# Rectifying the experts' first layer through a 32-bit buffer in SBUF, and scaling a routing table on another engine

## The chip, the cores and the metric

The kernel runs on one core of one Trainium2 chip. The metric is the device time of one execution in microseconds (us). Before the change it is 1554.09 us, the median of 3 runs (1553.83 to 1555.44). A core has a matrix engine (TensorE, shown as PE, its weight loads as PEld), a vector engine (VectorE, DVE), an engine for functions (ScalarE, ACT), a general one (GpSimd, POOL) and one that issues transfers (SyncE, SP). Each takes its own instructions strictly in order and waits for others by semaphores. SBUF is the working memory. TensorE writes its results to PSUM.

## What is computed

Attention with decay, then a dense layer pair, then a mixture of experts. Only the last matters here:

```python
logits = x @ w_gate                      # 4608 tokens, 8 experts
order = np.argsort(-logits.flatten())    # each token goes to the best expert that is not full (576 places)
for e in range(8):
    mask = assigned == e
    h = np.maximum(x[mask] @ w1[e], 0.0) # 576 x 1024
    out[mask] = h @ w2[e]                # 576 x 512
```

## The kernel before

The first two thirds of the time, to about 1016 us of the trace, are attention and the dense layers. The experts follow in `phase_c`. Matrix products are in 32 bits of which TensorE takes a shorter form (`fp32r`), so every factor is split into a high part (a copy into `fp32r`) and a low part (the value less its high part). A product is then three: high by high, low by high, high by low.

`experts(r)` (before: lines 1137 to 1200) does one expert, and is called for r from 0 to 7. Its first layer has eight steps f, one for 128 of the 1024 hidden columns. A step has 24 matmuls (L1158) into two PSUM buffers of 288 tokens each, `ps[0]` and `ps[1]`. These come from the pool `psF` with four buffers, so that step f+2 writes the buffers of step f. After its matmuls a step issues: two ACT instructions that rectify each half of PSUM straight into the high part `hh` (L1167); then `split_w(r, 2, f)`, which splits one block of the second layer's weights, the high part `w2h` by ACT (L1074) and the low part `w2l` by POOL (L1075). The low part of the rectified step is a function `low`, kept in the list `late`. It is called in the next step after the sixth matmul (j == 5), or after the eighth step. It issues three DVE instructions of 288, 224 and 64 columns (L1171), each of which reads PSUM again, rectifies, and subtracts `hh`. The second layer (L1189) uses `hh`, `hl`, `w2h` and `w2l` of f = 0 to 7 for each of five blocks of tokens; its results go to SBUF by ACT (L1194, L1196) and out by an indirect transfer on POOL.

While one expert is computed, the routing finds the tokens of a later one. `route(r)` is a generator whose pieces are issued between the matmuls of the experts: after each matmul pair a clock in the program is advanced by a constant (`TK1`, `TK2`), and a piece is issued when the clock has passed a time set by constants (`Y_...`). So the order on every engine is fixed when the program is built. A round of routing finds a threshold in six steps. A step compares on DVE (`cmp`, L839, L908 or L925), counts on PE (L930 or L934), goes on on DVE (`ca`, L938), on PE (L949, L950), and again on DVE (`d`, `dm`, `tr`, L957 to L960, whose result `pi` sets the next threshold). Then comes the choice of an expert (`GG`, L969; PE L973, L975; `nn`, `mx`, `X`, L979 to L988; PE L995) and the list of its tokens: a table `b1` (0 or 1, 128x720, bf16) by DVE (L1018), its product with a constant per partition, into one half of `R`, by ACT (L1019), a table `A` by DVE (L1021), the other half of `R` by DVE (L1023), and their products on PE (L1027). Routing 0 comes before the first expert; routings 1 to 7 lie beside experts 0 to 6.

`SB` holds small tables of the routing in one PSUM bank (its tile is named `st` in the trace), and `F` constants in SBUF (`tf`).

Of the kernel before, what the change touches and what calls it, by code (L numbers as in the profile page):

```python
# [9 lines left out]
F32 = mybir.dt.float32  # L10
# [8 lines left out]
AF = mybir.ActivationFunctionType  # L19
OP = mybir.AluOpType  # L20
# [6 lines left out]
E, FE, CAP = 8, 1024, 576  # L27
# [721 lines left out]
def phase_c(tc, ctx, w1, w2, rtf, rti, rth, rtb, x2d, L, out):  # L749
    nc = tc.nc  # L750
# [3 lines left out]
    fp = ctx.enter_context(tc.tile_pool(name="fp", bufs=1))  # L754
# [4 lines left out]
    V = nc.vector  # L759
# [7 lines left out]
    F = {k: tf[:, a:b] for k, (a, b) in RF.items()}  # L767
# [4 lines left out]
    def bc(ap, axis, n):  # L772
        shape = list(ap.shape)
        shape.insert(axis, n)
        return ap.unsqueeze(axis).to_broadcast(shape)

    def rt(shape, dt, name, bufs=1):
        return rp.tile(shape, dt, tag=name, name=name, bufs=bufs)
# [62 lines left out]
    def route(r):  # L841
# [29 lines left out]
        if r < E - 1:  # L871
# [6 lines left out]
            for half in range(2):  # L878
# [7 lines left out]
                for s, (shift, J) in enumerate(STEPS):  # L886
# [58 lines left out]
                    for i in range(nj):  # L945
                        o = pd[:, 8 * nc_ * i:8 * nc_ * i + 8 * nc_]
# [8 lines left out]
                    if not fast:  # L955
# [5 lines left out]
                                           op0=OP.is_ge, op1=OP.mult, accum_out=pi)  # L961
# [54 lines left out]
        b1 = rt([128, NCOL, 20], BF16, "b1")  # L1016
        R = rt([128, NCOL, 2, 20], BF16, "R")
        V.tensor_tensor(b1, bc(zh, 2, 20), bc(F["i20"], 1, NCOL), op=OP.is_equal)  # L1018
        nc.scalar.activation(R[:, :, 1, :], b1, AF.Copy, scale=F["p"])  # L1019
        yield Y_Z  # L1020
        V.tensor_tensor(A, bc(zl, 2, 32), bc(F["i32"], 1, NCOL), op=OP.is_equal)  # L1021
        yield 1.4
# [42 lines left out]
    def load_w2(r, f):  # L1065
        if f < 8:
            WS[r, 2, f] = wp.tile([128, KC, 128], F32, tag="ws2", name="ws2", bufs=3)
            nc.sync.dma_start(out=WS[r, 2, f], in_=w2[bass.ds(EV[r], 1), f].rearrange("e p k m -> (e p) k m"))

    def split_w(r, i, f):  # L1070
        s = WS.pop((r, i, f))
        h = wp.tile([128, KC, 128], F32R, tag=f"w{i}h{f}", name=f"w{i}h{f}")
        l = wp.tile([128, KC, 128], F32R, tag=f"w{i}l{f}", name=f"w{i}l{f}")
        nc.scalar.activation(h, s, AF.Copy)  # L1074
        nc.gpsimd.tensor_tensor(l, s, h.bitcast(F32), op=OP.subtract)  # L1075
        (W1 if i == 1 else W2)[f] = h, l
# [42 lines left out]
    def each(f):  # L1119
        for r in range(E):  # L1120
            for d in f(r):
                yield d

    threads = [[0.0, each(f)] for f in (route, weights, tokens)]
    clock = [0.0]

    def tick(dt):
        clock[0] += dt
        for th_ in threads:
            while th_[1] is not None and th_[0] <= clock[0]:  # L1130
                d = next(th_[1], None)
                if d is None:
                    th_[1] = None
                else:
                    th_[0] = clock[0] + d * (YS[len(IDX) > 1] if th_ is threads[0] else YS[0])

    def experts(r):
        while r not in XT:
            tick(0.2)
        xh, xl = XT.pop(r)  # L1140
        idx = IDX[r]
        H, late = [], []
        load_w2(r, 0)
        load_w2(r, 1)
        for f in range(8):
            load_w2(r, f + 2)
            ps = [psF.tile([128, 512], F32, tag="ff", name="ff")[:, :288] for _ in range(2)]
            while f not in W1:
                tick(0.2)
            w1h, w1l = W1.pop(f)  # L1150
            prods = [(w, xh, k) for k in range(KC) for w in (w1h, w1l)] + [(w1h, xl, k) for k in range(KC)]
            seq = [(i, u) for i in range(12) for u in range(2)]
            if r == 0 and f == 0:

                seq = [(i, u) for a, b in ((0, 8), (8, 12)) for u in range(2) for i in range(a, b)]
            for j, (i, u) in enumerate(seq):
                w, x, k = prods[i]
                nc.tensor.matmul(ps[u], w[:, k, :], x[:, k, 288 * u:288 * u + 288], start=i == 0, stop=i == 11)  # L1158
                if j % 2:
                    tick(TK1)  # L1160
                if late and j == 5:
                    late.pop()()

            hh = fp.tile([128, CAP + 64], F32R, tag=f"hh{f}", name="hh")
            hl = fp.tile([128, CAP - 64], F32R, tag=f"hl{f}", name="hl")
            for u in range(2):
                nc.scalar.activation(hh[:, 288 * u:288 * u + 288], ps[u], AF.Relu)  # L1167

            def low(ps=ps, hh=hh, hl=hl):
                for a, b, o in ((0, 288, hl[:, :288]), (288, 512, hl[:, 288:]), (512, 576, hh[:, 576:])):  # L1170
                    V.scalar_tensor_tensor(o, ps[a // 288][:, a % 288:a % 288 + b - a], 0.0, hh[:, a:b].bitcast(F32),  # L1171
                                           op0=OP.max, op1=OP.subtract)
            late.append(low)
            H.append((hh, hl))
            split_w(r, 2, f)
            first_done[r] = f == 7
        late.pop()()
        for t in (0, 4, 1, 2, 3):
            n = min(128, CAP - 128 * t)
            ps = psF.tile([128, 512], F32, tag="ff", name="ff")  # L1180
            for f in range(8):
                w2h, w2l = (w.rearrange("p k m -> p (k m)") for w in W2[f])
                hh = H[f][0][:, 128 * t:128 * t + 128]
                if t < 4:
                    prods = (ps, hh, w2h), (ps, H[f][1][:, 128 * t:128 * t + 128], w2h), (ps, hh, w2l)
                else:
                    prods = (ps, hh, w2h), (ps[:n], hh[:, :n], w2l)
                for i, (o, h, w) in enumerate(prods):
                    nc.tensor.matmul(o, h, w, start=f == 0 and i == 0, stop=f == 7 and i == len(prods) - 1,  # L1189
                                     skip_group_check=t == 4)  # L1190
                    tick(TK2)
            o = fp.tile([128, DM], F32, tag="o", name="o", bufs=3)
            if t < 4:
                nc.scalar.activation(o, ps, AF.Copy)  # L1194
            else:
                nc.scalar.activation(o[:n], ps[n:], AF.Copy)  # L1196
                V.tensor_tensor(o[:n], ps[:n], o[:n], op=OP.add)
            nc.gpsimd.indirect_dma_start(out=out, out_offset=bass.IndirectOffsetOnAxis(ap=idx[:n, t:t + 1], axis=0),
                                         in_=o[:n], in_offset=None)
# [20 lines left out]
    for r in range(E):  # L1220
        experts(r)
# [82 lines left out]
```

## Time and profile before

| what | value |
|---|---|
| median of 3 runs | 1554.09 us (1553.83 to 1555.44) |
| the profiled execution | 1556.99 us, its span 1555.1 us, so 1.9 us around it |
| PE, share of the span | 94%, 1456.5 us |
| DVE | 73%, 1132.7 us |
| ACT | 49%, 761.5 us |
| POOL | 36%, 558.3 us |
| chain that ended last: PE, DVE, issue, ACT, POOL | 73%, 14%, 4%, 3%, 2% |
| mean granted TensorE clock | 0.973 of full speed |

The profile shows one execution. Busy time is the time in which an engine had an instruction under way; the chain that ended last is followed back from the last instruction to whatever released each one. In the views below a row names the line, the engine, the operation, what it writes and reads (`hl<-ff,hh`), partitions by elements and types, and how many there were.

### The profile page before, as it was taken

Reading aid. Unit: us, or ns where it says so; the run is one execution under the profiler, and the core shown is the slowest. Engines: PE = TensorE matmul, PEld = TensorE weight load, DVE = VectorE, ACT = ScalarE, POOL = GpSimd, SP = SyncE. Lnnn points to the kernel's source line nnn. Section 1 sums busy time; section 2 is a strip of 40 time slices with the busy share of each in tenths; the row PEclk is TensorE's granted clock in tenths of the full one; section 3 lists DMA queues with packets and bytes.
Section 4 is the critical chain, followed back from the end, with each engine's and each line's share of the span. In section 5 each row is a group of like instructions: output and inputs, shape, how many; then the busy total and the mean of one; then the engine's idle time right before and its main releaser. Section 6 shows DMA issues by size and latency. Waiting matters only on the chain.

```text
span 1555.1 us, 26174 instructions
## 1 busy us (share of the span) xinstructions
PE 1456.5 (94%) x9500; PEld 1276.3 (82%) x9500; DVE 1132.7 (73%) x2740; ACT 761.5 (49%) x1585; POOL 558.3 (36%) x492
## 2 busy tenths in 40 slices
PE   5989899899999999999999999937999999999997
PEld 4777788789898989898989898825788887887996
DVE  7999965878787878777878787867776766765210
ACT  4767775455656565656564646503333323323421
POOL 4546541212222221212121223224535535446541
PEclk7999999999999999999999999967999999999999
DMA  7522222111111111111111100013423423426210
GB/s 258 197 72 82 82 104 74 43 62 42 62 41 62 42 62 42 62 41 62 42 54 50 43 22 21 1 37 129 125 85 124 129 85 120 130 84 193 91 65 31
DMA packets 48610, 122.43 MB, mean 79 GB/s; under 512 B 6624, under 2 KB 13408, under 8 KB 48224
## 3 DMA queue, kind: packets, MB, share of 16 engines
q1 hardware_dynamic: 41184, 99.80, 19.2%
q0 software_dynamic: 6144, 19.93, 4.0%
q8 instruction: 75, 1.23, 0.3%
q10 hardware_dynamic: 1152, 1.02, 0.2%
q14 instruction: 55, 0.45, 0.1%
HBM read 101.85 MB, written 18.87 MB: 78 GB/s over the span
## 4 chain that ended last, share of the span: by engine, by line
PE 73%; DVE 14%; issue 4%; ACT 3%; POOL 2%; DMA 1%; SPq 0%; POOLq 0%; DVEq 0%; ACTq 0%
PE h L426 22%; PE x L489 21%; PE ff L1189 11%; PE ff L1158 10%; PE pb L290 2%; PE pb L357 2%; PE pb L369 1%; DVE work L208 1%; DVE t L456 1%; DVE t L450 1%; DVE junk L530 1%; DVE t L452 1%; PE tp L1112 1%; PE pb L305 1%; DVE h L454 1%
## 5 line engine op out<-in xcount | busy, mean ns | idle before, releaser
L470 POOL TENSOR_TENSOR gl<-t,gh 128x384 fp32r<-128x384 f32 x192 | 200.2, 1043 | 652.6 <-ACT gh L467 565.8
L426 PE MATMUL h<-xh,w0h 128*128 128x384 f32 x704 | 240.4, 341 | 11.8 <-DVE t L456 11.6
L426 PE MATMUL h<-xh,w0l 128*128 128x384 f32 x704 | 238.3, 338 | 0.0
L436 ACT ACTIVATE S<-h 128x384 f32<-128x384 f32 x192 | 93.7, 488 | 286.7 <-PE h L426 286.5
L489 PE MATMUL x<-w1h,gh 128*128 128x512 f32 x576 | 231.2, 401 | 0.5 <-ACT gh L467 0.5
L489 PE MATMUL x<-w1l,gh 128*128 128x512 f32 x576 | 226.9, 394 | 0.0
L489 PE MATMUL x<-w1h,gl 128*128 128x512 f32 x576 | 217.0, 395 | 1.3 <-POOL gl L470 1.0
L450 DVE SCALAR_TENSOR_TENSOR t<-t,S 128x384 f32<-128x384 f32 x192 | 114.1, 594 | 128.7 <-ACT t L439 128.1
L530 DVE SCALAR_TENSOR_TENSOR junk<-x2r,wg 128x512 f32<-128x512 f32 x240 | 168.7, 703 | 5.2
L426 PE MATMUL h<-xl,w0h 128*128 128x384 f32 x704 | 152.6, 338 | 0.0
L426 PEld LDWEIGHTS h<-xh,w0h 128*128 128x128 f32 x704 | 132.7, 188 | 23.4 <-DVE t L456 12.3
L1075 POOL TENSOR_TENSOR w2l<-ws,w2h 128x512 fp32r<-128x512 f32 x64 | 82.6, 1293 | 161.4 <-ACT w2h L1074 161.4
L426 PEld LDWEIGHTS h<-xh,w0l 128*128 128x128 f32 x704 | 133.1, 189 | 6.7
L489 PEld LDWEIGHTS x<-w1h,gl 128*128 128x128 f32 x576 | 108.1, 188 | 29.7 <-POOL gl L470 5.7
L1189 PE MATMUL ff<-w2h,hh 128*128 128x512 f32 x320 | 127.5, 399 | 3.1 <-DVE hl L1171 2.0
L456 DVE COPY_PREDICATED t<-m,h 128x384 f32<-128x384 uint16 x192 | 114.4, 596 | 20.9 <-ACT m L445 1.7
L1189 PE MATMUL ff<-w2l,hh 128*128 128x512 f32 (+1 forms) x320 | 127.4, 398 | 0.6 <-POOL w2l L1075 0.6
L489 PEld LDWEIGHTS x<-w1h,gh 128*128 128x128 f32 x576 | 108.6, 188 | 22.9 <-ACT gh L467 1.3
L426 PEld LDWEIGHTS h<-xl,w0h 128*128 128x128 f32 x704 | 126.7, 189 | 0.3 <-DVE xl L413 0.2
L439 ACT ACTIVATE t<-S,bias 128x384 f32<-128x384 f32 x192 | 118.3, 616 | 17.4 <-POOL gl L470 0.9
L489 PEld LDWEIGHTS x<-w1l,gh 128*128 128x128 f32 x576 | 108.6, 189 | 17.1
L1158 PE MATMUL ff<-xh,w1h 128*128 128x288 f32 x512 | 115.0, 302 | 6.3 <-DVE hl L1171 5.5
(212 smaller groups left out, 2989.6 us busy)
## 6 DMA issues: line engine op xcount, KB each, us to landing
ws<-in_w SPq DMA_DIRECT2D x128, 256.0 KB, 2.8
ain<-in_qkv SPq DMA_DIRECT2D x36, 768.0 KB, 4.2
wst<-in_wio SPq DMA_DIRECT2D x32, 512.0 KB, 3.5
x2d<-x2r SPq DMA_DIRECT2D x33, 256.0 KB, 2.0
w1h<-in_qkv SPq DMA_DIRECT2D x12, 192.0 KB, 4.6
w1l<-in_qkv SPq DMA_DIRECT2D x12, 192.0 KB, 3.5
w0h<-in_qkv SPq DMA_DIRECT2D x12, 192.0 KB, 4.0
w0l<-in_qkv SPq DMA_DIRECT2D x12, 192.0 KB, 4.1
```

The lines of the kernel that those rows point to most:

```text
L290: nc.tensor.matmul(PSA[k][a][:, chunk(c)], kt[r, chunk(c)], q[r, chunk(c)], start=True, stop=True)
L426: nc.tensor.matmul(h[:, :TB], w[0][f][:, hp, :], x, start=i == 0, stop=i == 11)
L436: nc.scalar.activation(S, h, AF.Square, scale=KSC)
L439: nc.scalar.activation(AT[s][2], AT[s][1], AF.Square, bias=bias[:, 0:1])
L450: nc.vector.scalar_tensor_tensor(t, t, PA - PB * PB / 4, S, op0=OP.add, op1=OP.mult)
L456: nc.vector.copy_predicated(t, m.bitcast(U16), h)
L470: nc.gpsimd.tensor_tensor(G[s][1], TT.pop(s), G[s][0].bitcast(F32), op=OP.subtract)
L489: nc.tensor.matmul(X2[n][i], g[:, i * 128:i * 128 + 128], w, start=(f == 0 and g is gh and w is wh), stop=(f == NF - 1 and g is gl))
L530: nc.vector.scalar_tensor_tensor(j, r, 1.0, wg[e // 4][:, e % 4, :], op0=OP.mult, op1=OP.mult, accum_out=L[:, c, e:e + 1])
L1075: nc.gpsimd.tensor_tensor(l, s, h.bitcast(F32), op=OP.subtract)
L1158: nc.tensor.matmul(ps[u], w[:, k, :], x[:, k, 288 * u:288 * u + 288], start=i == 0, stop=i == 11)
L1189: nc.tensor.matmul(o, h, w, start=f == 0 and i == 0, stop=f == 7 and i == len(prods) - 1, skip_group_check=t == 4)
```

## The change

In the first layer the two ACT instructions write 32-bit values to a new SBUF tile `raw` (two buffers). A third ACT instruction copies all 576 columns of it to the high part. `low` then is two DVE instructions, of 512 and 64 columns, which subtract `hh` from `raw`; they no longer read PSUM. In the routing, for every round but the first, the product of `b1` with a constant per partition goes from ACT to DVE.

```diff
@@ route
         V.tensor_tensor(b1, bc(zh, 2, 20), bc(F["i20"], 1, NCOL), op=OP.is_equal)
-        nc.scalar.activation(R[:, :, 1, :], b1, AF.Copy, scale=F["p"])
+        if r:
+            V.tensor_scalar(R[:, :, 1, :], b1, F["p"], None, op0=OP.mult)
+        else:
+            nc.scalar.activation(R[:, :, 1, :], b1, AF.Copy, scale=F["p"])
@@ experts
             hl = fp.tile([128, CAP - 64], F32R, tag=f"hl{f}", name="hl")
+            raw = fp.tile([128, CAP], F32, tag="raw", name="raw", bufs=2)
             for u in range(2):
-                nc.scalar.activation(hh[:, 288 * u:288 * u + 288], ps[u], AF.Relu)
-
-            def low(ps=ps, hh=hh, hl=hl):
-                for a, b, o in ((0, 288, hl[:, :288]), (288, 512, hl[:, 288:]), (512, 576, hh[:, 576:])):
-                    V.scalar_tensor_tensor(o, ps[a // 288][:, a % 288:a % 288 + b - a], 0.0, hh[:, a:b].bitcast(F32),
-                                           op0=OP.max, op1=OP.subtract)
+                nc.scalar.activation(raw[:, 288 * u:288 * u + 288], ps[u], AF.Relu)
+            nc.scalar.activation(hh[:, :CAP], raw, AF.Copy)
+
+            def low(raw=raw, hh=hh, hl=hl):
+                for a, b, o in ((0, 512, hl), (512, 576, hh[:, 576:])):
+                    V.tensor_tensor(o, raw[:, a:b], hh[:, a:b].bitcast(F32), op=OP.subtract)
             late.append(low)
```

The order of PE, POOL and SP is the same as before. ACT has 57 instructions more (64 copies, less 7 products of the routing). DVE has 57 fewer (64 less, 7 more).

DVE in expert 1, the low part of step f = 4 between two pieces of the routing (`ca` and `d`). Before:

```order
L938 TENSOR_TENSOR ca<-rt,tf 128x32
L1171 SCALAR_TENSOR_TENSOR hl<-ff,hh 128x288
L1171 SCALAR_TENSOR_TENSOR hl<-ff,hh 128x224
L1171 SCALAR_TENSOR_TENSOR hh<-ff,hh 128x64
L957 TENSOR_REDUCE d_12053<-rt 128x16
```

And with the change:

```order
L938 TENSOR_TENSOR ca<-rt,tf 128x32
L1176 TENSOR_TENSOR hl<-raw,hh 128x512
L1176 TENSOR_TENSOR hh<-raw,hh 128x64
L957 TENSOR_REDUCE d_12066<-rt 128x16
```

The place in the queue is the same; two instructions stand for three, and both operands are now in SBUF.

ACT at the end of expert 1's first layer (steps f = 6 and 7). Before:

```order
L1167 ACTIVATE hh<-ff 128x288 x2
L1074 ACTIVATE w2h_12158<-ws_11966 128x512
L1019 ACTIVATE R<-b_12189,tf 128x36x20
L1167 ACTIVATE hh<-ff 128x288 x2
L1074 ACTIVATE w2h_12218<-ws_12026 128x512
```

And with the change:

```order
L1171 ACTIVATE raw<-ff 128x288 x2
L1172 ACTIVATE hh<-raw 128x576
L1077 ACTIVATE w2h_12174<-ws_11979 128x512
L1171 ACTIVATE raw<-ff 128x288 x2
L1172 ACTIVATE hh<-raw 128x576
L1077 ACTIVATE w2h_12235<-ws_12040 128x512
```

The routing's product is gone from ACT's queue, where it stood ahead of step 7's rectifying; a copy stands between rectifying and the weights' split.

DVE at the same place, around the tables of the routing. Before:

```order
L1018 TENSOR_TENSOR b_12189<-st,tf 128x720
L1171 SCALAR_TENSOR_TENSOR hl<-ff,hh 128x288
L1171 SCALAR_TENSOR_TENSOR hl<-ff,hh 128x224
L1171 SCALAR_TENSOR_TENSOR hh<-ff,hh 128x64
L1171 SCALAR_TENSOR_TENSOR hl<-ff,hh 128x288
L1171 SCALAR_TENSOR_TENSOR hl<-ff,hh 128x224
L1171 SCALAR_TENSOR_TENSOR hh<-ff,hh 128x64
L1021 TENSOR_TENSOR A<-st,tf 128x1152
L1023 TENSOR_TENSOR R<-b_12189,st 128x36x20
```

And with the change:

```order
L1018 TENSOR_TENSOR b_12205<-st,tf 128x720
L1020 TENSOR_SCALAR R<-b_12205,tf 128x36x20
L1176 TENSOR_TENSOR hl<-raw,hh 128x512
L1176 TENSOR_TENSOR hh<-raw,hh 128x64
L1176 TENSOR_TENSOR hl<-raw,hh 128x512
L1176 TENSOR_TENSOR hh<-raw,hh 128x64
L1024 TENSOR_TENSOR A<-st,tf 128x1152
L1026 TENSOR_TENSOR R<-b_12205,st 128x36x20
```

The product now stands right behind the table that it reads, ahead of the low parts of steps 6 and 7.

## Rows read from the trace of the kernel before

**Rows 1.** Busy time by stage: engine busy us (instructions), granted clock, DMA share, GB/s

```profile
1120.00:1160.00 40.00, 38.64 (x311) 33.91 (x310) 26.77 (x81) 11.25 (x25) 16.33 (x15) 1.00 0.29 89
```

**Rows 2.** Waits of PE from 1075 us: us in total, times, longest

```profile
PE ff L1158 <- DVE hl L1171: 5.5, 6, 2.0
PE ff L1189 <- DVE hl L1171: 2.0, 2, 1.1
PE tp L1112 <- DVE xl L1115: 1.4, 1, 1.4
PE ff L1189 <- ACT w2h L1074: 1.1, 1, 1.1
```

**Rows 3.** Waits of ACT from 1075 us: us in total, times, longest

```profile
ACT hh L1167 <- PE ff L1158: 122.2, 53, 3.9
...
ACT R L1019 <- DVE b L1018: 33.0, 7, 6.8
```

**Rows 4.** Groups by shape from 1060 us: count | busy us, mean ns | idle before

```profile
L1167 ACT ACTIVATE hh<-ff 128x288 fp32r<-128x288 f32 x128 | 45.6, 408 | 125.6 <-PE ff L1158 125.5
L1074 ACT ACTIVATE w2h<-ws 128x512 fp32r<-128x512 f32 x64 | 40.6, 634 | 0.0
...
L1171 DVE SCALAR_TENSOR_TENSOR hl<-ff,hh 128x288 fp32r<-128x288 f32 x64 | 29.0, 453 | 58.9 <-ACT hh L1167 58.9
...
L1115 DVE TENSOR_TENSOR xl<-tp,xh 128x512 fp32r<-128x512 f32 x32 | 21.6, 687 | 26.9 <-ACT xh L1114 22.2 <-issue 3.1 <-ACT R L1019 1.5
```

**Rows 5.** Single lines over the span: count: ns min/median/max, first and last start

```profile
L450 DVE SCALAR_TENSOR_TENSOR t<-t,S x192: 537/555/1674, 48.0 to 1009.2; 128x384 f32<-128x384 f32 x192
...
L470 POOL TENSOR_TENSOR gl<-t,gh x192: 1000/1018/1524, 53.2 to 1012.4; 128x384 fp32r<-128x384 f32 x192
...
L1075 POOL TENSOR_TENSOR w2l<-ws,w2h x64: 1278/1293/1323, 1077.5 to 1521.6; 128x512 fp32r<-128x512 f32 x64
```

**Rows 6.** DVE and POOL in order of time, near 126 us: start and length, us

```profile
125.73 0.68 DVE L226 SCALAR_TENSOR_TENSOR work<-wst,work 128x512 f32<-128x512 f32 x1
126.13 1.17 POOL L470 TENSOR_TENSOR gl<-t,gh 128x384 fp32r<-128x384 f32 x1 [2.93 <-ACT gh L467]
126.34 1.51 DVE L237 TENSOR_TENSOR w1l<-work,w1h 128x512 fp32r<-128x512 f32 x1
```

**Rows 7.** The same view near 121 us and near 208 us

```profile
120.60 1.02 POOL L470 TENSOR_TENSOR gl<-t,gh 128x384 fp32r<-128x384 f32 x1
120.62 1.41 DVE L450 SCALAR_TENSOR_TENSOR t<-t,S 128x384 f32<-128x384 f32 x1 [1.74 <-ACT t L439]
...
208.34 0.68 DVE L226 SCALAR_TENSOR_TENSOR work<-wst,work 128x512 f32<-128x512 f32 x1
208.38 1.52 POOL L470 TENSOR_TENSOR gl<-t,gh 128x384 fp32r<-128x384 f32 x1 [1.42 <-issue]
```

**Rows 8.** In order of time, expert 1, step f = 4 of the first layer

```profile
1154.16 0.71 ACT L1167 ACTIVATE hh<-ff 128x288 fp32r<-128x288 f32 x2 [2.52 <-PE ff L1158]
1154.61 0.76 DVE L1171 SCALAR_TENSOR_TENSOR hl<-ff,hh 128x288 fp32r<-128x288 f32 x2 [0.49 <-ACT hh L1167]
...
1155.48 1.28 POOL L1075 TENSOR_TENSOR w2l<-ws,w2h 128x512 fp32r<-128x512 f32 x1 [2.46 <-ACT w2h L1074]
...
1155.98 0.23 DVE L957 TENSOR_REDUCE d<-rt 128x16 f32<-128x64 f32 x1 [0.48 <-PE rt L950]
...
1157.70 0.75 DVE L969 TENSOR_TENSOR GG<-P,st 128x576 bf16<-128x576 bf16 x1
...
1158.81 0.42 PE L973 MATMUL rt<-GG,tb 128*128 128x192 bf16 x3
```

**Rows 9.** In order of time, the end of expert 1's first layer

```profile
1165.24 0.90 ACT L1019 ACTIVATE R<-b,tf 128x720 bf16<-128x720 bf16 x1 [2.91 <-DVE b L1018]
...
1168.53 0.89 DVE L1023 TENSOR_TENSOR R<-b,st 128x720 bf16<-128x720 bf16 x1
...
1170.56 0.66 PE L1027 MATMUL rt<-R,A 128*128 128x160 bf16 x7
```

## The prediction

> **What bounds the kernel now.** I read the stages first. In the stretch of the experts, PE is busy 38.6 of 40 us, DVE 26.8, ACT 11.3 and POOL 16.3, with the clock granted in full [rows 1]. So PE sets the time there, and a change on the other engines counts only through PE's waits. I read these next. From 1075 us on PE waits 5.5 + 2.0 us for `hl`, the low part whose reading of PSUM sets a buffer free, 1.4 us for `xl`, and 1.1 us for `w2h` [rows 2]: 10.0 us, nearly all that the change could remove. Behind most of it stands one thing: ACT waits 33.0 us, in seven places, with the routing's product at the head of its queue until DVE has made the table `b1` [rows 3], and the rectifying of the next step waits behind it. The reader is to see that the change aims at these waits. What it can cost has to come from the routing: its pieces on DVE and PE are interleaved in a fixed order with the experts, so a DVE that runs late stops PE at the next routing matmul.
>
> **What the change does, part by part.**
>
> *ACT.* 64 copies of 576 columns are added. A copy of 512 takes 634 ns [rows 4], so I take 0.7 us each, some 45 us in all (0.63 to 0.75 us each is the bound). They are hidden in throughput: ACT waits 122.2 us for the first layer's matmuls before it rectifies, in 53 places [rows 3]. They are not hidden in delay: `hh`, and so the low part, is ready 0.8 us later (0.7 and a wait of about 0.1 us of ACT for its own result). Where that cover is gone, which is where the routing's product now stands, the product leaves too. `w2h` and with it POOL's `w2l` also come 0.8 us later. PE waited for `w2h` once, 1.1 us [rows 2], where ACT was held by the routing's product; else the 21 matmuls of steps 0 to 6 of the second layer stand ahead of step 7's weights. I cost the delay at nothing; without that cover it would be 0.8 us in each of 8 experts, 6.4 us.
>
> *PSUM.* A buffer is free when ACT has rectified it, no longer when DVE has subtracted. The 7.5 us of waits for `hl` lose their reason. ACT now waits for DVE if `raw`'s two buffers are full, one whole step later than PE did. What is late next is DVE.
>
> *DVE's low part.* Three instructions become two. The old ones cost 453 ns for 288 columns, and by 687 ns for 512 [rows 4] a column is about 1.04 ns. A subtraction of 512 columns that has both operands in SBUF takes 0.68 us undisturbed [rows 6], 64 columns more by that slope 0.2. So the work is about the same. The Trainium skill ("VectorE: DVE Perf Modes", The TRN2 errata) prices a result from SBUF at 58 cycles and its columns, from PSUM at 120; by that the large part would take an estimated 0.59 us and run 0.06 us shorter than from PSUM, where the rows show 0.68 against 0.69. The rows decide; by the page the 64-column part would start before POOL's `w2l`, and the sum would be that of the second rival below.
>
> *The port.* This is the point on which the forecast rests. A DVE instruction that reads two operands from SBUF is stopped by a POOL instruction that does so, and stops it. L450 takes 555 ns at the median and up to 1674, POOL's L470 1018 and up to 1524; `w2l`, in the experts, where the low parts read PSUM, never leaves 1278 to 1323 [rows 5]. The order decides: DVE that starts 20 ns after POOL takes 1.41 us, DVE that starts 40 ns before it makes POOL take 1.52 [rows 7]. Between two DVE instructions that follow each other POOL gets in: one began at 125.73, POOL at 126.13 took 0.15 us more than its 1.02 (so the first held it for 0.55 us), and the second, 0.61 us after the first, ended 0.55 us after POOL [rows 6]. The Trainium skill says this too ("SBUF — State Buffer", Who interferes with whom): the shared port goes to whichever instruction starts first, for its whole length; it speaks against this change, and the trace agrees.
>
> *One step worked out.* Expert 1, step 4 [rows 8]: the two rectifyings end at 1154.87. The copy ends at C = 1155.65. The 512-column part starts 0.04 us later (the first rectifying, 408 ns [rows 4], ends at 1154.57, and DVE started at 1154.61), so at 1155.69; the 64-column part 0.61 us behind it at C + 0.65. `w2l` came 0.61 us after the rectifyings and now comes at C + 0.61, 0.04 us before the 64 columns. By [rows 7] POOL wins, and DVE stands until 1155.65 + 0.61 + 1.29 + 0.1 = 1157.65. Behind it stands `d`, before at 1155.98: 1.67 us late. From `d` to the end of `GG` is 2.47 us, so `GG` ends at 1160.1; PE came for it at 1158.81. PE stops for 1.3 us.
>
> *The sum of the stops.* I went through the 48 low parts of experts 0 to 5 in this way, each from where DVE stood behind the rectifying. 33 cost nothing: DVE's next instruction waited for PE anyway, or PE came over 1 us later. The others, in us: expert 0: 1.3, 1.7, 2.1; expert 1: 0.3, 1.3, 1.0; expert 2: 1.1, 0.8, 0.4; expert 4: 0.9, 1.3, 1.0; expert 5: 0.7, 0.4, 0.3. Together 14.6 us. Experts 6 and 7 have no routing in their first layers, and DVE idles there: nothing.
>
> *The routing's product.* DVE has no such row; its cheapest neighbour would be some 0.3 us, its dearest is the other half of `R` at 0.89 [rows 9]. I take 0.6, as it has one operand in SBUF and no second. It frees ACT's queue, and PE would reach the end of a first layer earlier. But there the routing's own matmul L1027 comes, and DVE must have `A` and `R` ready. In expert 1 `R` ends at 1169.42 and PE takes it at 1170.56 [rows 9]: 1.1 us to spare. With the change the product and the two low parts, with step 7's `w2l` between the two halves, move `A` and `R` by 1.2 us, so nothing of PE's 1.6 us there is kept. By the same working the places at L1027 give, in us: expert 0 -0.9, 1 +0.1, 2 +0.6, 3 -1.6, 4 -0.2, 5 +0.3, and the wait for `xl` in expert 6 -1.0. Together -2.7.
>
> *Sum.* 14.6 - 2.7 = 11.9 us more. On the profiled execution of 1556.99 us that is 1568.9; it lies 2.9 us above the median of the three runs, so I forecast **1566 us**. The stops are uncertain by about half a microsecond each in common, and the product by 0.3 us in six places, so this case spans 1558 to 1574.
>
> **The rivals.**
>
> *The 64 columns slip in first.* The margin is 0.04 us, and DVE 40 ns ahead wins [rows 7]. Then the common case costs only the copy's delay, most of which PE's lateness covers. There remain 3.8 us of stops, where the low part starts late and falls into `w2l`, against about 3.7 us gained: 1554 us, 1551 to 1558. For it: the margin is no larger than what I can read. Against it: two instructions that follow each other let POOL in [rows 6].
>
> *No stop at the port worth speaking of, and the waits go.* If POOL's start misses the low part (because ACT splits the weights later than I think, or DVE gets the 64 columns through as part of the first) and the routing has more slack than I read, the 10.0 us of [rows 2] go, less 1.5 us for the copy's delay and about 2.5 us which the routing's own matmuls take back: 6 us less, 1548, 1544 to 1551. It decides from the point where the low part ends no later than about 1 us after it does now. For it: PE's waits are real, and PSUM is freed without DVE. Against it: [rows 5], where the same two engines stop each other by up to a whole instruction.
>
> **How the numbers follow.** A measurement of this kernel can tell about 0.2% from no change, 3.1 us. The forecast has 0.60, all of it slower by more than that. The first rival has 0.20: 0.14 within, 0.04 slower, 0.02 faster. The second has 0.20: 0.19 faster, 0.01 within. So faster 0.21, same 0.15, slower 0.64. The range of 1548 to 1573 leaves out about half of the second rival and a little of the forecast's upper end.
>
> **What would show it.** Right: `w2l` still near 1.29 us, but the 64-column subtraction with a median far over 0.2 us, near 1.3 where DVE was free; waits of PE for `GG`, `cmp` and `X` of the routing in place of those for `hl`; ACT's 33.0 us wait gone; L1027 waiting for `R`. Wrong: subtractions of 0.68 and 0.2 us throughout; waits of PE for the routing no longer than now; or `w2l` stretched to 1.9 us, which would mean that DVE goes first. The forecast falls if the 64 columns are not held in most steps.

## The result, and the profile after

The changed kernel takes 1568.86 us (median of 5 runs, 1567.58 to 1570.11), the kernel before on the same chip 1554.77 (1553.83 to 1555.82): 1.0088 times as long, 95% interval 1.0075 to 1.0102. It is slower by 14.1 us.

The part that the change touches runs from the first to the last matmul `ff`. It took 475.4 us before (1070.4 to 1545.8 us) and takes 490.7 us now (1066.9 to 1557.6), 15.3 us more; the part ahead of it, which the change leaves as it is, was 3.5 us shorter in this execution (over the twelve traces of this case the first `ff` starts at 1064.8 to 1070.4 us). One stretch of it by stages, which answers to [rows 1] and has its columns:

```profile
1120.00:1160.00 40.00, 38.05 (x317) 33.86 (x316) 29.94 (x75) 15.99 (x32) 15.61 (x15) 1.00 0.27 86
```

DVE does fewer instructions than before (75 for 81) and is busy for 29.94 us, where it was 26.77. So its instructions have become longer. Which ones, the view of single lines says (as [rows 5]; L1176 is the low part, L1020 the product, L1172 the copy, L1078 the weights' low part):

```profile
L1176 DVE TENSOR_TENSOR hl<-raw,hh x64: 679/692/1794, 1074.3 to 1533.4; 128x512 fp32r<-128x512 f32 x64
L1176 DVE TENSOR_TENSOR hh<-raw,hh x64: 210/1311/1339, 1074.9 to 1534.1; 128x64 fp32r<-128x64 f32 x64
L1020 DVE TENSOR_SCALAR R<-b,tf x7: 407/407/421, 1106.9 to 1435.8; 128x720 bf16<-128x720 bf16 x7
L1172 ACT ACTIVATE hh<-raw x64: 682/686/688, 1073.6 to 1532.7; 128x576 fp32r<-128x576 f32 x64
L1078 POOL TENSOR_TENSOR w2l<-ws,w2h x64: 1265/1287/1813, 1074.9 to 1534.0; 128x512 fp32r<-128x512 f32 x64
```

64 columns take 210 ns undisturbed and 1311 at the median, more than the 512 columns ahead of them and as long as one `w2l` of POOL, whose own median has not moved. The place worked out ahead, expert 1's step f = 4, shows why; in order of time, as [rows 8]:

```profile
1153.61 0.71 ACT L1171 ACTIVATE raw<-ff 128x288 f32<-128x288 f32 x2 [2.61 <-PE ff L1161]
...
1154.36 0.69 ACT L1172 ACTIVATE hh<-raw 128x576 fp32r<-128x576 f32 x1
...
1155.08 0.69 DVE L1176 TENSOR_TENSOR hl<-raw,hh 128x512 fp32r<-128x512 f32 x1 [1.51 <-ACT hh L1172]
...
1155.64 1.29 POOL L1078 TENSOR_TENSOR w2l<-ws,w2h 128x512 fp32r<-128x512 f32 x1 [3.28 <-ACT w2h L1077]
1155.68 1.33 DVE L1176 TENSOR_TENSOR hh<-raw,hh 128x64 fp32r<-128x64 f32 x1
...
1156.93 0.21 DVE L957 TENSOR_REDUCE d<-rt 128x16 f32<-128x64 f32 x1
```

POOL starts 0.04 us ahead of the 64 columns and ends at 1156.93; these end 0.08 us behind it, at 1157.01. Behind them stand `d` and the rest of the routing. What this does to PE shows in its waits from 1075 us (as [rows 2]; not shown is a last row of 0.3 us for `xl`):

```profile
PE rt L1030 <- DVE R L1026: 12.9, 6, 3.7
PE rt L934 <- DVE cmp L925: 4.0, 5, 1.5
PE rt L973 <- DVE GG L969: 3.4, 4, 1.0
PE rt L930 <- DVE P L863: 1.7, 3, 1.3
PE rt L930 <- DVE cmp L839: 1.0, 1, 1.0
PE rt L930 <- DVE cmp L925: 0.8, 1, 0.8
PE rt L995 <- DVE ei L990: 0.4, 2, 0.2
```

No wait for `hl` is left, nor one for `w2h` or `w2l`, nor the 1.0 us for a transfer that PE waited before. In their place PE waits for the routing, 24.2 us in all, above all for `R`. On ACT the 33.0 us for `b1` of [rows 3] are gone, and the rectifying waits nearly only for the first layer's matmuls (not shown: 4.9 us once for DVE, by the profile for `im` of the routing, and 1.7 us once for a low part):

```profile
ACT raw L1171 <- PE ff L1161: 108.8, 59, 4.0
```

The longest wait for `R` stands at the end of expert 1's first layer, as [rows 9]:

```profile
1166.67 0.41 DVE L1020 TENSOR_SCALAR R<-b,tf 128x720 bf16<-128x720 bf16 x1
...
1166.99 0.68 DVE L1176 TENSOR_TENSOR hl<-raw,hh 128x512 fp32r<-128x512 f32 x1
...
1167.43 1.40 POOL L1078 TENSOR_TENSOR w2l<-ws,w2h 128x512 fp32r<-128x512 f32 x1 [2.38 <-ACT w2h L1077]
...
1167.59 1.32 DVE L1176 TENSOR_TENSOR hh<-raw,hh 128x64 fp32r<-128x64 f32 x1
...
1168.80 5.41 POOL L1078 TENSOR_TENSOR w1l<-ws,w1h 128x512 fp32r<-128x512 f32 x4
1168.84 1.79 DVE L1176 TENSOR_TENSOR hl<-raw,hh 128x512 fp32r<-128x512 f32 x1
...
1170.56 1.28 DVE L1176 TENSOR_TENSOR hh<-raw,hh 128x64 fp32r<-128x64 f32 x1
1171.76 1.34 DVE L1024 TENSOR_TENSOR A<-st,tf 128x1152 bf16<-128x1152 int32 x1
1173.02 0.89 DVE L1026 TENSOR_TENSOR R<-b,st 128x720 bf16<-128x720 bf16 x1
...
1173.96 0.80 PE L1030 MATMUL rt<-R,A 128*128 128x160 bf16 x9 [3.69 <-DVE R L1026]
```

Three of the four subtractions are held here, for 1.1 us each: one by `w2l`, two by the `w1l` of the next expert's weights, which POOL does four at a stretch. PE stands until 1173.96 for a table that was ready at 1169.42 before.

And there is a second loss behind the stop. Busy time, granted clock (the third number from the end) and transfers around it, in stretches of 2 us (columns as in [rows 1]):

```profile
1170.00:1172.00 2.00, 0.27 (x2) 0.00 (x0) 2.00 (x3) 0.61 (x1) 2.00 (x3) 1.00 0.96 339
1172.00:1174.00 2.00, 0.04 (x1) 0.13 (x2) 1.97 (x3) 0.00 (x0) 2.00 (x2) 1.00 0.88 338
1174.00:1176.00 2.00, 2.00 (x13) 1.72 (x13) 1.84 (x8) 0.00 (x0) 0.20 (x1) 0.65 0.08 30
1176.00:1178.00 2.00, 2.00 (x6) 1.28 (x5) 0.20 (x1) 1.83 (x4) 0.96 (x1) 0.50 0.00 0
1178.00:1180.00 2.00, 2.00 (x13) 1.30 (x12) 0.89 (x4) 0.32 (x1) 1.97 (x3) 1.00 0.34 131
```

PE stood for 3.69 us with the clock granted in full (2.4 GHz), and when it went on it was granted half (1.2 GHz): six matmuls in 2 us. From 1174.54 to 1178.05 eight matmuls of 512 columns started 0.43 us apart, from then on 0.23, so 1.7 us were lost here.

### The profile page after: what moved, and what is told of

The parts are those of the page before. It is cut to its first block, busy times and chain, and to the rows that moved or that the text cites. A ratio compares the mean times of both kernels' runs of the same rounds, so it can differ in the third digit from the quotient of the medians.

```text
span 1567.0 us, 26176 instructions
## 1 busy us (share of the span) xinstructions
PE 1459.2 (93%) x9500; PEld 1280.9 (82%) x9500; DVE 1181.2 (75%) x2683; ACT 801.0 (51%) x1642; POOL 561.4 (36%) x492
## 4 chain that ended last, share of the span: by engine, by line
PE 70%; DVE 22%; ACT 4%; issue 2%; DMA 1%; POOL 0%; ACTq 0%; POOLq 0%; SPq 0%; DVEq 0%
PE h L426 21%; PE x L489 21%; PE ff L1193 11%; PE ff L1161 7%; PE pb L290 2%; DVE hl L1176 2%; PE pb L357 2%; DVE hh L1176 2%; PE pb L369 1%; DVE cmp L925 1%; DVE work L208 1%; DVE t L456 1%; PE tp L1115 1%; DVE junk L530 1%; DVE t L450 1%
## 5 line engine op out<-in xcount | busy, mean ns | idle before, releaser
L426 PE MATMUL h<-xh,w0h 128*128 128x384 f32 x704 | 240.0, 341 | 12.3 <-DVE t L456 12.2
L1078 POOL TENSOR_TENSOR w2l<-ws,w2h 128x512 fp32r<-128x512 f32 x64 | 85.1, 1330 | 163.9 <-ACT w2h L1077 163.9
L452 DVE TENSOR_TENSOR t<-t,h 128x384 f32<-128x384 f32 x192 | 106.1, 553 | 19.6 <-ACT m L445 1.4
```

Source lines behind the costliest of these rows:

```text
L426: nc.tensor.matmul(h[:, :TB], w[0][f][:, hp, :], x, start=i == 0, stop=i == 11)
L452: nc.vector.tensor_tensor(t, t, h, op=OP.mult)
```

## The experiments

Theory: the two subtractions read two operands from SBUF, and POOL's weight splits hold them; DVE runs late, and PE waits for the routing instead of for `hl`. Rivals: the copy makes everything 0.8 us later and that is what PE pays; the product is what makes `R` late; or the early release of PSUM was worth nothing from the start. Each ratio below is against the kernel before on the same chip, with its 95% interval.

### The product on DVE: left out, and alone

```diff
@@ e1_raw_only: the change, but
-        if r:
-            V.tensor_scalar(R[:, :, 1, :], b1, F["p"], None, op0=OP.mult)
-        else:
-            nc.scalar.activation(R[:, :, 1, :], b1, AF.Copy, scale=F["p"])
+        nc.scalar.activation(R[:, :, 1, :], b1, AF.Copy, scale=F["p"])
@@ e2_product_only: the kernel before, but
-        nc.scalar.activation(R[:, :, 1, :], b1, AF.Copy, scale=F["p"])
+        if r:
+            V.tensor_scalar(R[:, :, 1, :], b1, F["p"], None, op0=OP.mult)
+        else:
+            nc.scalar.activation(R[:, :, 1, :], b1, AF.Copy, scale=F["p"])
```

Expected of the first:

> The change with the routing's product left on ACT. Theory (the stops come from POOL's w2l holding DVE between the two subtractions, C): the 64-column subtraction keeps its median near 1.3 us, the stops of PE at the counting matmuls stay near the 10 to 13 us of the change, and ACT again stands about 33 us for the table: 1563 to 1573 us, most likely 1568. Rival (the product on DVE is what makes R late, as L1030 alone waits 12.9 us): the wait at the table falls to about 1 us and the time to 1555 to 1560.

Expected of the second:

> The kernel before with only the routing's product on DVE for rounds 1 to 7; the low parts read PSUM as before. Theory: ACT's 33 us wait for the table and most of PE's waits for hl go (about 10 us), a part of it is given back at the matmul of R: 1548 to 1553 us, most likely 1550. Rival (the product on DVE makes R late): 1558 or more, with PE waiting over 5 us for R.

The first took 1583.98 us, 1.0186 (1.0172 to 1.0200), which is above all that was expected. PE's and ACT's waits in it (L1027 is the routing's own matmul here, L1158 and L1190 the two layers):

```profile
PE rt L1027 <- DVE R L1023: 13.3, 5, 4.3
PE ff L1158 <- ACT raw L1168: 4.4, 2, 2.3
...
PE ff L1190 <- ACT raw L1168: 2.1, 1, 2.1
...
ACT R L1019 <- DVE b L1018: 34.8, 7, 6.0
```

PE waits for `R` as long as with the change (13.3 for 12.9 us), so the product does not make `R` late: that rival falls. But ACT stands 34.8 us for `b1` with a rectifying behind it, and now it is the rectifying that frees PSUM. The buffer comes free later, not earlier, at these places, and PE waits 4.4 + 2.1 us for it. Against the change, PE in the experts' part is idle 9.2 us longer (35.2 for 26.0) and busy 6.0 us longer (470.7 for 464.7), at a mean granted clock of 0.97 for 0.98.

The second took 1547.67 us, 0.9953 (0.9939 to 0.9967), 7 us faster than before, 0.3 us under the range that was expected. So this part of the change is worth 7 us by itself and 15 beside the other part (1583.98 to 1568.86), and the other part costs 29 by itself and 21 beside this one.

### The 64 columns first

```diff
@@ e3_small_first: the change, but
-                for a, b, o in ((0, 512, hl), (512, 576, hh[:, 576:])):
+                for a, b, o in ((512, 576, hh[:, 576:]), (0, 512, hl)):
```

> The change with the two subtractions in the other order, 64 columns first, nothing else. Theory (C): where DVE is free the 64 columns are done before w2l comes, and the 512 columns have the port before it; the low part ends 1.1 us earlier, w2l takes some 0.15 us longer, PE's stops at the counting matmuls fall from about 13 to 3 to 6 us: 1556 to 1563 us. Rival (the 0.8 us of the copy, A, make the routing late, not the port): no difference, 1567 to 1570.

1555.22 us, 1.0000 (0.9991 to 1.0009): the same two instructions in the other order win back 13.6 of the 14.1 us, a little more than was expected. The work, the copy and the place in DVE's queue are the same; only the start of the 512 columns is now ahead of `w2l`. Single lines:

```profile
L1176 DVE TENSOR_TENSOR hh<-raw,hh x64: 210/225/1322, 1075.4 to 1520.4; 128x64 fp32r<-128x64 f32 x64
L1176 DVE TENSOR_TENSOR hl<-raw,hh x64: 677/684/1795, 1075.5 to 1520.5; 128x512 fp32r<-128x512 f32 x64
L1078 POOL TENSOR_TENSOR w2l<-ws,w2h x64: 1262/1401/1816, 1075.9 to 1520.9; 128x512 fp32r<-128x512 f32 x64
```

The 64 columns take 225 ns, the 512 684, and it is POOL that is held now (1401 for 1287). The copy's delay alone can therefore not be the main cost. PE still waits 10.2 us for `R`, where some of the low parts meet the next expert's `w1l`.

### The low part from PSUM again, with copy and product kept

```diff
@@ e4_low_from_psum: the change, but
-            def low(raw=raw, hh=hh, hl=hl):
-                for a, b, o in ((0, 512, hl), (512, 576, hh[:, 576:])):
-                    V.tensor_tensor(o, raw[:, a:b], hh[:, a:b].bitcast(F32), op=OP.subtract)
+            def low(ps=ps, hh=hh, hl=hl):
+                for a, b, o in ((0, 288, hl[:, :288]), (288, 512, hl[:, 288:]), (512, 576, hh[:, 576:])):
+                    V.scalar_tensor_tensor(o, ps[a // 288][:, a % 288:a % 288 + b - a], 0.0, hh[:, a:b].bitcast(F32),
+                                           op0=OP.max, op1=OP.subtract)
```

> The change (raw, the copy, the product on DVE) with the low parts again three instructions that read PSUM and hh, so as late as in the change by the copy but with one operand in SBUF. Theory (C): none of them is stopped by w2l, all three keep 0.45, 0.38 and 0.21 us; the stops at the counting matmuls fall to 1 to 4 us, waits for hl come back in part as PSUM is freed by the low part: 1551 to 1558 us. Rival (A, the copy's delay): the stops stay, 1564 or more.

1553.99 us, 0.9994 (0.9984 to 1.0004), as expected. The 64 columns, which have one operand in SBUF here, are never held, and `w2l` keeps its length:

```profile
L1176 DVE SCALAR_TENSOR_TENSOR hh<-ff,hh x64: 206/214/217, 1075.6 to 1518.2; 128x64 fp32r<-128x64 f32 x64
...
L1078 POOL TENSOR_TENSOR w2l<-ws,w2h x64: 1276/1289/1310, 1075.5 to 1518.1; 128x512 fp32r<-128x512 f32 x64
```

Its waits on PE:

```profile
PE ff L1161 <- DVE hl L1176: 4.7, 6, 1.7
...
PE ff L1194 <- DVE hl L1176: 2.4, 2, 1.7
```

The waits for `hl` are back (7.1 us, before 7.5), those for `R` as small as before (0.4, before 0.3). Against `e2_product_only` this kernel differs only by `raw` and the copy, and takes 6.3 us more: that is what the copy costs while PSUM waits for the low part.

### Eleven low parts from PSUM, or eleven from SBUF

The worst places for `R` lie between the product and the table's other half. There 11 of the 64 low parts are issued; `e5_psum_at_table` reads PSUM for these and SBUF for the other 53, and `e6_raw_at_table` the other way round (`if not table["open"]`).

```diff
@@ e5_psum_at_table: the change, but
+            table["open"] = True          # behind the product
+        table["open"] = False             # ahead of the other half of R
@@
+                if table["open"]:
+                    for a, b, o in ((0, 288, hl[:, :288]), (288, 512, hl[:, 288:]), (512, 576, hh[:, 576:])):
+                        V.scalar_tensor_tensor(o, ps[a // 288][:, a % 288:a % 288 + b - a], 0.0, hh[:, a:b].bitcast(F32),
+                                               op0=OP.max, op1=OP.subtract)
+                else:
+                    for a, b, o in ((0, 512, hl), (512, 576, hh[:, 576:])):
+                        V.tensor_tensor(o, raw[:, a:b], hh[:, a:b].bitcast(F32), op=OP.subtract)
```

Expected of the one and of the other:

> The change, but the low parts that stand on DVE between the routing's product and the table's other half (11 of 64) read PSUM with three instructions; the other 53 read raw. Theory (low parts held there by w2l and by the next expert's w1l make R late): PE's wait for R falls from 12.9 us to at most 4, the stops at the counting matmuls stay at about 10: 1556 to 1562 us. Rival (R is late because the counting before it was): the wait for R stays over 9 us, 1566 or more.

> The complement: only those 11 low parts read raw in SBUF, the other 53 read PSUM. Theory: the stops at the counting matmuls fall to 1 to 5 us as with all low parts from PSUM, PE's wait for R is 7 to 12 us: 1559 to 1565 us. Rival: the wait for R is under 3 us and the time that of all low parts from PSUM, 1552 to 1556.

The first was expected to win back the waits for `R`, and did not: 1568.33 us, 1.0087 (1.0073 to 1.0101), no faster than the change. Three rows of PE's waits:

```profile
PE ff L1165 <- DVE hl L1181: 5.6, 3, 2.0
...
PE ff L1202 <- DVE hl L1181: 3.7, 2, 2.0
...
PE rt L1034 <- DVE R L1029: 0.3, 1, 0.3
```

The wait for `R` fell from 12.9 to 0.3 us as expected, but 9.3 us of waits for `hl` came back. DVE is late at these places in either form, and PE meets it at the next thing it needs: with PSUM held by the low part that is the buffer, with PSUM free it is `R`. The second kernel took 1556.79 us, 1.0017 (1.0008 to 1.0026), with 10.9 us of waits for `R`; that wait is as expected, the time 2 us under its range:

```profile
PE rt L1034 <- DVE R L1029: 10.9, 6, 3.1
```

Set against `e4_low_from_psum`, which reads PSUM everywhere, the eleven alone cost 3.6 us (0.9994 to 1.0017) and the 53 alone 14.5 (0.9994 to 1.0087), as much as all 64 together (0.9994 to 1.0088). So the large row, `R`, is not the large cost: with the eleven reading PSUM, PE waits at these places for `hl` in its place.

### POOL without reads

The last question is whether it is really the reading of POOL, not its being busy. Here POOL fills `w2l` with zeros in the first kernel, and in the second multiplies `w2h` by zero, with one operand from SBUF (POOL's subtraction has two); the low part of the second layer's weights is left out in both.

```diff
@@ e8_pool_writes_only and e8b_pool_one_operand: the change, but
-        nc.gpsimd.tensor_tensor(l, s, h.bitcast(F32), op=OP.subtract)
+        if i == 1:
+            nc.gpsimd.tensor_tensor(l, s, h.bitcast(F32), op=OP.subtract)
+        else:
+            nc.gpsimd.memset(l.bitcast(F32), 0.0)
@@ e8b has as its last line
+            nc.gpsimd.tensor_scalar(l, h.bitcast(F32), 0.0, None, op0=OP.mult)
```

> The change, with POOL filling the low part of the second layer's weights with zeros in place of subtracting: that part of the computation is left out, POOL reads no SBUF there and does not wait for the high part. PE, ACT and DVE have the same work. Theory (C): the 64-column subtraction takes 0.21 us and the 512 columns 0.68 in nearly all steps outside the next expert's w1l, PE's stops at the counting matmuls fall to 1 to 5 us: 1546 to 1556 us. Rival (any POOL instruction under way holds DVE, or the lateness comes from the copy): the 64 columns stay near 1.3 us or the time above 1562.

> The change, with POOL multiplying the high part of the second layer's weights by zero in place of subtracting it (left out as in the last): it still waits for the high part, so it starts 0.04 us ahead of the 64 columns, but reads one operand from SBUF. If reading at all holds DVE: the 64 columns are held for as long as this instruction lasts, and if that is over 0.6 us the time stays over 1558. If only a second operand does: 0.21 us, and 1546 to 1556.

With zeros written: 1542.70 us, 0.9937 (0.9923 to 0.9950), below the range that was expected. With the fill in place of the subtraction the change is a gain of 11 us; with the subtraction it is a loss of 14. The 64 columns, first here and then in the second kernel, where POOL's row follows:

```profile
L1179 DVE TENSOR_TENSOR hh<-raw,hh x64: 214/218/1319, 1074.4 to 1507.8; 128x64 fp32r<-128x64 f32 x64
```

```profile
L1179 DVE TENSOR_TENSOR hh<-raw,hh x64: 208/648/1318, 1075.4 to 1514.3; 128x64 fp32r<-128x64 f32 x64
L1081 POOL TENSOR_SCALAR w2l<-w2h x64: 1489/1492/1987, 1075.3 to 1514.3; 128x512 fp32r<-128x512 f32 x64
```

The median is 218 ns with the fill. With one operand read it is 648, though that POOL instruction lasts 1492 ns; the kernel took 1549.06 us, 0.9971 (0.9959 to 0.9983). The fill needs no `w2h` and starts earlier, so the first kernel also takes POOL, its `w1l` too, out of step with the low parts: its 11 us say what POOL's meeting them costs, not what a fill would save that came at the subtraction's time. That POOL's reading counts and not its being busy is shown by fewer cases: five of the 64 short ones begin 0.01 to 0.23 us after the start of a fill, and all five take 0.22 us, while the two that were held (1.32 us) met a subtraction for `w1l`. In the second kernel POOL starts where the subtraction did, mostly 0.03 to 0.04 us ahead of the short ones. They are held for 0.43 us, where the subtraction held them for 1.09: the multiplication with one operand costs less than the subtraction with two. Neither case that was expected came about, a hold as long as the instruction or none; the time is in the range of the second.

### The low part called earlier

If the low part reads PSUM, PE's waits for `hl` fall when it is called earlier in the next step. Both kernels are `e2_product_only` with one number changed:

```diff
@@ e7_product_low_earlier (3) and e9_product_low_second (1)
-                if late and j == 5:
+                if late and j == 3:
```

> The kernel before with the product on DVE, and the low part called after the fourth matmul of the next step in place of the sixth; a try for a faster version. PSUM is freed a little earlier where DVE's queue has routing work between: the 5.6 us of waits for hl fall to 3 to 5, the routing is pushed behind by as much in some places: 1544 to 1549 us, most likely 1547. If the order between low part and routing does not matter: no difference from 1547.7.

> As the faster version (product on DVE, low parts from PSUM), the low part called after the second matmul of the next step: 1542 to 1547 us if the earlier place goes on helping, 1545 to 1549 if DVE now stands waiting for ACT's rectifying with routing work behind it, which is what I expect: most likely 1545.

They took 1544.07 us, 0.9935 (0.9921 to 0.9948), and 1543.74 us, 0.9938 (0.9925 to 0.9952): no different from each other, and about 10 us faster than the kernel before and 25 faster than the change. About 7 of the 10 are the product's; for the 3 of the earlier call the intervals with `e2_product_only` (0.9939 to 0.9967) still overlap. The waits for `hl` that are left in the first:

```profile
PE ff L1161 <- DVE hl L1174: 1.9, 4, 1.1
```

So most of what the change was after, 7.5 us of waits for `hl`, is to be had without a buffer: take the product out of ACT's queue and call the low part earlier.

## Why the prediction was right, point by point

The forecast was 1566 us, slower, with a range of 1548 to 1573; measured were 1568.86. The sum was 11.9 us more, and the difference of the medians is 14.1. The direction and the mechanism are what the runs show; that the sum came so near is luck, as two of its terms were wrong by 4.7 and 5.0 us in opposite directions.

- **Port: right.** POOL was to start 0.04 us ahead of the 64 columns, and did (1155.64 and 1155.68). They are held to POOL's end in 38 of the 64 steps (median 1311 ns). The margin was thin, as the first rival said: in 28 steps `w2l` starts 0.03 to 0.07 us ahead of the 64 columns, and these are held; in one it starts 0.024 us ahead, and they take 0.22 us. `e3_small_first` shows that the order decides, `e4_low_from_psum` that it takes two operands of DVE in SBUF, and `e8b_pool_one_operand` that it depends on what POOL does at that moment. The Trainium skill ("SBUF — State Buffer", Who interferes with whom) has the pair of ports locked by whoever comes first; by that rule, 1.29 us of POOL hold the 64 columns for what is left of it, and the rows of the change agree. With one operand on POOL's side they don't: 648 ns within an instruction of 1492.
- **The step worked out: right.** The 64 columns were to end 2.0 us after the copy; they end at 1157.01, 1.96 after it (1155.05). PE's stop was put at 1.3 us; it waited 1.03 for `GG`, at 1159.45.
- **The sum of the stops: 14.6 us, too large.** PE's waits at the counting and the choice add up to 11.3 us, less 1.4 in the same rows of before: 9.9. By experts, from the first matmul of one to that of the next, the 11.3 are 3.7 us in expert 0 where 5.1 were worked out, then 1.9 for 2.6, 1.0 for 2.3, 0.2 for none, 3.2 for 3.2 and 1.4 for 1.4 (sums; the single stops were not matched). The sizes were too large in experts 0 to 2, by up to 1.5 us in an expert.
- **The places at `R`: -2.7 us, too small by 5.** PE waits there 12.9 us, before 0.3; gone are 10.3 (7.5 for `hl`, 1.1 for `w2h`, 0.6 for `w2l`, 1.1 of the 1.4 for `xl`): 12.6 less 10.3, +2.3. Half of it is expert 1, where these waits are 2.6 us more than before and 0.1 was worked out. The step that failed there is the count of the holds: I let `w2l` hold one subtraction at the end of the layer, and did not see that the next expert's `w1l` would hold two more. That made a stop of 3.69 us. (The 1.6 us that I took for PE's wait there before are 1.1 in the trace.) Experts 2, 4 and 5 add 0.6 to 0.8 us each to what was worked out; in expert 5 no low part is held between the product and `R`, so what makes `R` late there lies ahead of the product and was not separated.
- **The clock: not in the sum.** The two errors cancel (9.9 + 2.3 = 12.2 for 11.9). Less the 1.0 us of waiting for a transfer that is gone too, that is 11.2; counted without the rows, PE's idle time in the experts' part grew by 11.8 us (26.0 for 14.2). The rest goes with PE's busy time there, 464.7 us for 461.2, at a mean granted clock of 0.98 for 1.00: 11.8 and 3.5 make the 15.3 us. That the clock would fall behind a stop was no term of mine.
- **The product: 0.6 us priced, 0.41 measured.** It costs nothing that shows, and takes off 7 us alone.
- **The copy: nothing priced for its delay; not shown here, wrong where the low part holds PSUM.** There it costs 6.3 us (`e4_low_from_psum` against `e2_product_only`). With the change PSUM is free by then, but no run has the change without the copy; that with POOL's fill it is 11 us faster than before only says that the delay is not what costs the 14. 0.7 us each was right: 686 ns. The 0.1 us that ACT was to wait for its own result had no row, and measured 0.03.
- **The low part's work: right.** 512 columns from SBUF take 679 to 692 ns undisturbed, and the run with POOL's fill has 218 ns for 64 columns at the median. The Trainium skill's table ("VectorE: DVE Perf Modes", The TRN2 errata) made an estimated 0.59 us of the 512; right below it the same section has 691 ns, measured, for an addition of two fp32 tensors of 512 columns. The prediction passed that over; the runs agree with it. The prediction also put the table's case to its second rival; 64 columns that start ahead of `w2l` are its first.
- **First rival (the 64 columns slip in, 1554): did not happen.** Forced by the order of the two subtractions it gives 1555.22, near its price; there the 64 columns start first of all, which is not quite the rival's case.
- **Second rival (no stop at the port, 1548): did not happen, and was priced too high.** With POOL's fill it is 1542.70. The product alone takes off 7 us, more than the rival gave to all; the rest was not separated.

Not tried: PSUM freed early without any subtraction of two operands from SBUF. The kernel's pools already hold eight PSUM buffers in this part, and a ninth was not tried.

## What to carry to other kernels

Before an operand of a DVE instruction is moved from PSUM to SBUF, look at what POOL reads from SBUF at that moment: 10.3 us of waits were removed here, and 22.5 (24.2 less the 1.7 that these rows had before) put in their place, by two instructions that do the same work in the same place of the queue. If they cannot be kept apart, put the short one first, so that the long one is under way when POOL arrives. And a buffer that comes free earlier is worth something only if the engine that freed it is not late for the next thing too: ask where the waiter will meet it again, as it met DVE at `R`, and try the plain reordering (the product off the queue, the low part earlier) ahead of a new buffer.

## What the runs showed of the hardware that was not expected

- A POOL instruction with one operand from SBUF, 1.49 us long, held the 64 columns for 0.43 us only (648 ns for 218): in all 41 cases they ended 0.80 to 0.81 us before it did. It did not hold at all those that came 1.07 us or more behind its start (0.21 to 0.22 us). One with two operands, 1.29 us long, held them for 1.09 (1311), to its end.
- PE's clock falls behind a stop. In the stretch shown with the result PE had been busy for 2.00 of the 2 us to 1170, stood 3.69 us, and then ran for 3.5 us at 1.2 GHz. In the experts' part there are, apart from a low clock at the first matmul in every trace, four such falls with the change (each some 3.5 to 4 us long, at half of the full clock), none in the kernel before, two with the 64 columns first, four in `e5_psum_at_table`, and none in `e4_low_from_psum`. What brings one is open, and the length of a stop does not tell it: with the change one followed a stop of 1.51 us (at 1092.1), in `e3_small_first` none followed one of 2.42 us (at 1167.5), and the longest stop is 2.0 us both in `e5_psum_at_table` and in the kernel before. So a stop of PE can cost more than its length, 1.7 us more in expert 1.
